# Storing the kept input gradient from GpSimd's queue in a planned S4 and FFN gradient kernel

## The chip, the cores and the metric

The kernel runs on one core of a Trainium2 chip, in one launch. The metric is the device time of a run in microseconds. Before the change three runs took 560.41, 562.75 and 563.41 us, so the median is 562.75.

## The reference

The reference is a small network and all its gradients. The input `A_u` (2048 rows of 512) is normalized; one branch is an S4 layer (a long convolution whose kernel comes from a complex diagonal recurrence, done with Fourier transforms), the other a feed-forward layer with 1792 inner columns; one gates the other.

```python
def _A_ref(u, A_re, A_im, B_re, B_im, C_re, C_im, log_dt, Dskip):
    dt = jnp.exp(log_dt)[:, None]
    A = A_re + 1j * A_im
    ...
    P = jnp.exp(logdA[:, :, None] * l[None, None, :])
    K = jnp.einsum("dn,dnl,dn->dl", Cc, P, dB).real
    ...
    return y + u * Dskip[None, None, :]      # y: u convolved with K, by FFT

def _B_ref(x, w1, w2):
    h = _silu(jnp.einsum("bsd,df->bsf", x, w1))
    return jnp.einsum("bsf,fd->bsd", h, w2)

xn = _layernorm(A_u)
out = A_u + _A_ref(xn, ...) * _silu(_B_ref(xn, B_w1, B_w2))

_out, _vjp = jax.vjp(_f, A_u, A_A_re, ..., A_Dskip, B_w1, B_w2)
return (out, *_vjp(grad_out))
```

The outputs are `out` and eleven gradients: those of the input, of the eight S4 parameter arrays and of the two weights.

## The kernel before

**How an order comes about.** The program is written twice. `body` runs once against a `Recorder`, which only notes each operation (so most operations have line L171, the line that emits them). `Plan` reads the recorded list, finds what depends on what, gives each operation a cost, and plays the engines forward; at each moment the ready operation with the smallest key goes next on its engine. The keys come from a backward pass (`backward`, how long before the end each operation is due), `ROUNDS` rounds of forward and backward from a start of noise named by `FROM`, and then from `NUDGES`, a list of small random shifts of keys that a search has kept. `FIRST` and `LAST` are the settings of `forward` in the rounds and in the last pass: in the signature of `forward` their five numbers are `hold`, `table`, `turn`, `shy` and `land`. A DMA is released no earlier than `latest[n] - hold`. ScalarE takes an operation whose activation table is loaded ahead of one whose table is not, as long as its key is less than `table` larger; `turn` does the same on TensorE for the form of the tiles. `shy` is what a copy must gain to leave its better engine, and `land` how long a transfer is taken to land. Then all operations are emitted in the order found, engine by engine, and each engine keeps that order.

**Copies without an engine.** Most copies out of PSUM are noted as `k.ev`, "any": the plan gives each to VectorE or to ScalarE.

**Stores.** `k.st` is a DMA start on GpSimd's queue (POOL); `k.nc.sync.dma_start` is one on SyncE's queue (SP). Both queues issue in their own order and stand still at an issue whose data or room is not ready.

**The stages**, in the names that the profile shows. *Head:* constants (`TF`, `TI`, `SEL`, `MK`, `FO`), `dt` and thirty exponentials `mag_all` on ScalarE, stored to `Md` by eight DMAs and reloaded as `mag`; the normalized rows `xn`, turned by TensorE into `XT`. The working area `AR` lies on the room of the head's tiles, so its first write waits for those eight stores. *Forward:* the S4 tables (`AR`, `sn`, `E`, `YD`, `W`, `Xr`, `KE`), four blocks of convolution by transforms (`ps_s` to `dA` forward, `ps_i` back, `S_b` the result) and the feed-forward layer (`ps_h` to `hT`, silu to `aT`, `ps_o` to `ob`). *Backward:* the gated rows are turned (`doT`), `gen_ffn_da` computes `ps_da` and `dhT` for eight chunks of 256 rows and then, for each chunk, two products `ps_dx`, the feed-forward share of the input's gradient; meanwhile `gen_conv_bwd` runs the transforms backward into `ds` and `gen_out` writes the first output (`go_x`). *Parameters:* `GE`, `Gb`, `ps_v`, `Vb`, `Tp`, `Tq` and `psS` are the S4 parameter gradients; `ps_w` the weight gradients, which read `hT` again as `h_in`. *End:* `gen_ln_bwd` joins the shares of the input's gradient through the normalization (`Gt`).

**Kept input gradient.** For the first `APART` = 5 chunks `ps_dx` cannot yet be added to `ds`. These ten tiles are copied to `pd_s` (one buffer) and stored in the DRAM tensor `Pd`; `gen_ln_bwd` reads them back as `pd_l`. For the other three chunks VectorE adds `ps_dx` to `ds` directly.

Of the kernel before, what the change touches and what calls it, by code (L numbers as in the profile page):

```python
# [180 lines left out]
class Plan:  # L181
# [5 lines left out]
    FROM, ROUNDS = (649172052, 1, 0), 5  # L187
    FIRST, LAST = (30000.0, 1500.0, 1500.0, 120.0, 3500.0), (30000.0, 1500.0, 1500.0, 120.0, 3500.0)
    NUDGES = [(2732807006, 5, 2000), (3483623756, 4, 500), (36678232, 7, 1000), (3625006935, 3, 100), (1835227684, 0, 100),
# [600 lines left out]
    def solve(self):  # L790
# [6 lines left out]
        for i in range(self.ROUNDS):  # L797
# [3 lines left out]
            if i < self.ROUNDS - 1:  # L801
                p = self.forward(key, latest, *self.FIRST)
        for seed, way, much in self.NUDGES:
            of = lambda n: self.noise(n, seed)
# [895 lines left out]
def gen_ffn_da(k, da):  # L1700
# [11 lines left out]
    for c in range(T // 2):  # L1712
# [26 lines left out]
        for t in range(2):  # L1739
# [4 lines left out]
            if c < k.apart:  # L1744
                pd = da.tile([P, D], BF16, name="pd_s", tag="pd_s", bufs=1)
# [326 lines left out]
```

## Time and profile before

| | |
|---|---|
| runs | 560.41, 562.75, 563.41 us, median 562.75 |
| the profiled execution's own time | 562.31 us |
| its span, first to last instruction | 560.6 us |
| mean granted TensorE clock | 0.991 |
| instructions | 14249 |

In a row of a group the columns are: line, engine, operation, output from input, size and type, count, then busy us and mean ns of one, then how long the engine stood idle before it and what ended that. In a timeline they are start and length in us. In the chain of waits they are start, length and what ran. An issue row gives the queue, the count, the size of one and the median us from issue to landing. PEld is the loading of weights into TensorE, beside the multiplication.

### The profile page before, as it was taken

The page shows a single profiled execution, that of the slowest core. Times are in us where ns is not written, and L with a number is a line of the kernel's source. Part 1 is how long each engine was busy: PE and PEld are TensorE (multiplying, and loading weights), DVE is VectorE, ACT ScalarE, POOL GpSimd, SP SyncE. Part 2 cuts the span into 40 slices and gives each one's busy share as a digit, 9 for nine tenths or more (in the row PEclk, how much of TensorE's full clock was granted, in tenths as well). Part 3 has the DMA queues.
Part 4 walks back from the last instruction along what each step waited for, and adds up shares of the span by engine and source line. Part 5 has one row for each costly group of instructions (what it writes and reads, how often), then busy time and mean ns, then how long its engine had stood idle before and what let it go on. Part 6 is the DMA issues. An engine that isn't in the chain of part 4 may idle for free.

```text
span 560.6 us, 14249 instructions
## 1 busy us (share of the span) xinstructions
PE 515.5 (92%) x5820; PEld 380.5 (68%) x5820; DVE 508.1 (91%) x866; ACT 432.0 (77%) x726; POOL 69.4 (12%) x138
## 2 busy tenths in 40 slices
PE   1698999999989997889999999999969999999997
PEld 1465677868657666565877667778657687778775
DVE  9989999999999799999999999649999999999932
ACT  8989899999989889989878878247367665785621
POOL 5131111100100100000000100000000303301142
PEclk9999999999999998999999999999989999999999
DMA  8996959997999999985498997997999999998893
GB/s 236 270 354 179 291 191 337 246 335 155 237 350 280 359 337 218 236 208 169 156 236 295 252 329 234 188 264 180 229 254 241 227 237 277 256 229 217 200 233 109
DMA packets 178882, 137.77 MB, mean 246 GB/s; under 512 B 125121, under 2 KB 158657, under 8 KB 176257
## 3 DMA queue, kind: packets, MB, share of 16 engines
q1 hardware_dynamic: 172384, 118.77, 82.5%
q0 software_dynamic: 6144, 17.83, 9.6%
q8 instruction: 45, 0.74, 0.5%
q10 hardware_dynamic: 288, 0.26, 0.2%
q14 instruction: 21, 0.16, 0.1%
HBM read 50.07 MB, written 56.63 MB: 190 GB/s over the span
## 4 chain that ended last, share of the span: by engine, by line
PE 58%; DVE 16%; ACT 13%; DMA 8%; issue 3%; SPq 2%; POOL 0%; DVEq 0%; ACTq 0%; POOLq 0%
PE ps_w L171 18%; PE ps_da L171 8%; PE ps_i L171 7%; PE ps_dx L171 6%; DMA dB<-dA 4%; PE ps_s L171 4%; PE ps_o L171 3%; ACT mag_all L171 3%; PE ps_h L171 3%; PE pt_t L171 3%; PE psS L171 3%; PE ps_v L171 2%; ACT dA L171 2%; DVE AR L171 2%; DVE dA L171 2%
## 5 line engine op out<-in xcount | busy, mean ns | idle before, releaser
L171 PEld LDWEIGHTS <-W 128*128 128x128 bf16 x952 | 88.1, 99 | 22.9 <-issue 7.4
L171 ACT CAST dA<-ps_s 128x512 bf16<-128x512 f32 x160 | 86.2, 641 | 9.2 <-PE ps_s L171 6.3
L171 PE MATMUL ps_o<-W,aT 128*128 128x512 bf16 x224 | 59.0, 379 | 2.9 <-ACT aT L171 2.9
L171 PEld LDWEIGHTS <-xn 128*128 128x128 bf16 x512 | 47.3, 99 | 20.1 <-DVE xn L171 13.0
L171 PE MATMUL ps_da<-doT,W 128*128 128x256 bf16 x448 | 59.7, 273 | 0.8 <-DVE doT L171 0.8
L171 PE MATMUL ps_h<-XT,W 128*128 128x256 bf16 x448 | 58.9, 277 | 1.3 <-DVE dA L171 0.8
L171 PE MATMUL ps_w<-YD,a_tok 128*128 128x512 bf16 x224 | 57.5, 382 | 0.0
L171 PE MATMUL ps_w<-dh_tok,xn 128*128 128x256 bf16 x448 | 57.1, 273 | 0.0
L171 ACT CAST Vb<-ps_v 128x336 bf16<-128x336 f32 x109 | 40.6, 459 | 21.2 <-PE ps_v L171 15.5
L171 PE MATMUL ps_dx<-W,dhT 128*128 128x512 bf16 x224 | 55.2, 379 | 0.0
L171 ACT CAST dB<-ps_i 128x512 bf16<-128x512 f32 x82 | 45.3, 647 | 4.5 <-PE ps_i L171 4.3
L171 DVE TENSOR_TENSOR dhT<-ps_da,dhT 128x512 bf16<-128x512 f32 x56 | 37.8, 685 | 6.1 <-PE ps_da L171 5.9
L171 PEld LDWEIGHTS <-TF 128*128 128x128 bf16 x416 | 28.5, 100 | 12.5 <-ACT TF L171 5.3
L171 PEld LDWEIGHTS <-YD 128*128 128x128 bf16 x576 | 28.4, 98 | 9.0 <-DVE YD L171 1.7
L171 PEld LDWEIGHTS <-dhT 128*128 128x128 bf16 x224 | 20.7, 98 | 20.1 <-issue 1.2
L171 PEld LDWEIGHTS <-a_tok 128*128 128x128 bf16 x224 | 21.3, 99 | 16.9 <-issue 0.5
L171 PEld LDWEIGHTS <-aT 128*128 128x128 bf16 x224 | 19.4, 98 | 19.5 <-ACT aT L171 3.4
L171 PE MATMUL ps_v<-Gb,YT 128*128 128x168 bf16 x256 | 31.1, 242 | 1.3 <-DVE Gb L171 0.7
L171 ACT CAST o<-ps_w 128x512 bf16<-128x512 f32 (+1 forms) x27 | 15.1, 559 | 20.9 <-PE ps_w L171 20.4
L171 PE MATMUL ps_s<-dB,F 128*64 128x512 bf16 x192 | 28.6, 400 | 2.8 <-DMA dB<-dA 1.7
L171 POOL DMA_DIRECT2D out_dram<-o x20 | 12.3, 616 | 142.8 <-ACT o L171 135.0
L171 ACT ACTIVATE sn<-AR 128x1920 bf16<-128x1920 int16 x16 | 28.7, 1870 | 0.0
(218 smaller groups left out, 1212.9 us busy)
## 6 DMA issues: line engine op xcount, KB each, us to landing
Yd<-YD SPq DMA_DIRECT2D x8, 1024.0 KB, 6.5
h_in<-Hd SPq DMA_DIRECT2D x11, 512.0 KB, 5.5
Ed<-E SPq DMA_DIRECT2D x8, 672.0 KB, 4.3
Eb<-Ed SPq DMA_DIRECT2D x8, 672.0 KB, 5.4
Hd<-hT POOLq DMA_DIRECT2D x8, 512.0 KB, 5.7
dhT<-Hd SPq DMA_DIRECT2D x8, 512.0 KB, 5.4
DHd<-dhT SPq DMA_DIRECT2D x8, 512.0 KB, 6.9
Md<-mag_all SPq DMA_DIRECT2D x8, 480.0 KB, 6.4
```

What stands on the lines that cost most here:

```text
L171: getattr(getattr(nc, engine), op)(*[on(a) for a in args], **{w: on(a) for w, a in kw.items()})
```

## The change

The store of `pd_s` goes through `k.st`, so from SP's queue to POOL's, and the plan's numbers are new: another start, four rounds instead of five, a `table` of 5000 instead of 1500, and 557 nudges instead of 663. The computation is the same.

```diff
@@ class Plan
-    FROM, ROUNDS = (649172052, 1, 0), 5
-    FIRST, LAST = (30000.0, 1500.0, 1500.0, 120.0, 3500.0), (30000.0, 1500.0, 1500.0, 120.0, 3500.0)
-    NUDGES = [(2732807006, 5, 2000), (3483623756, 4, 500), (36678232, 7, 1000), (3625006935, 3, 100), (1835227684, 0, 100),
...
+    FROM, ROUNDS = (99146811, 1, 1000), 4
+    FIRST, LAST = (30000.0, 5000.0, 1500.0, 120.0, 3500.0), (30000.0, 5000.0, 1500.0, 120.0, 3500.0)
+    NUDGES = [(1422119664, 3, 16000), (3699653561, 7, 2000), (2414858728, 4, 500), (342434683, 3, 4000), (3955565900, 7, 8000),
...
@@ gen_ffn_da
             if c < k.apart:
                 pd = da.tile([P, D], BF16, name="pd_s", tag="pd_s", bufs=1)
                 k.ev(pd[:], ps[:])
-                k.nc.sync.dma_start(k.Pd[:, 2 * c + t, :], pd[:])
+                k.st(k.Pd[:, 2 * c + t, :], pd[:])

**How it moves instructions.** Nearly every engine's order changes. Three places matter for what follows.

The first is the head on ScalarE, from the first table load to the exponentials. Before:

```order
L171 ACT_TABLE_LOAD
L171 ACTIVATE TF<-prod 128x2048
L171 ACT_TABLE_LOAD
L171 ACTIVATE dt<-ldt 128x512
L171 ACT_TABLE_LOAD
L171 ACTIVATE sf<-kf,mpi 128x128
L171 ACTIVATE sv<-kq,mpi 128x192
L171 ACT_TABLE_LOAD
L171 ACTIVATE mag_all<-lamr 128x8x64 x30
```

and with the change:

```order
L171 ACT_TABLE_LOAD
L171 ACTIVATE TF<-prod 128x2048 x2
L171 ACTIVATE sf<-kf,mpi 128x128
L171 ACTIVATE sv<-kq,mpi 128x192
L171 ACT_TABLE_LOAD
L171 ACTIVATE dt<-ldt 128x512
L171 COPY TI<-pt_t 128x1024
L171 ACTIVATE mag_all<-lamr 128x8x64 x30
```

The second `TF` and the sines now come ahead of the exponentials, two table loads stand in front of `mag_all` instead of four, and a `TI` copy has joined. On VectorE, what stands in front of `lamr`, which `mag_all` reads, was

```order
L171 TENSOR_SCALAR kq<-kk 128x64
L171 COPY TI<-pt_t 128x1024
L171 TENSOR_SCALAR kq<-kq 128x192
L171 TENSOR_SCALAR pj<-ip 128x1
L171 TENSOR_TENSOR lamr<-dt,par_Ar 128x512
```

and is

```order
L171 TENSOR_TENSOR rl<-xcst,pj 128x8
L171 COPY TI<-pt_t 128x1024
L171 TENSOR_TENSOR rl<-xcst,pj 128x12
L171 COPY TI<-pt_t 128x1024
L171 CAST rl<-pj 128x1
L171 TENSOR_TENSOR m_106<-pa,ia 128x4
L171 COPY TI<-pt_t 128x1024
L171 TENSOR_TENSOR MK<-rl,m_106 128x88
L171 TENSOR_TENSOR F_130<-sf,maskf 128x128
L171 TENSOR_TENSOR sv<-sv,maskf 128x192
L171 TENSOR_TENSOR lamr<-dt,par_Ar 128x512
```

so that two more `TI` copies and several small constants (three more `SEL` further up) now come first.

The second place is where the kept gradient is stored. On SP the first two of the ten stood so:

```order
L171 DMA dhT<-Hd 128x8x256
L171 DMA Pd<-pd_s 128x512
L171 DMA DHd<-dhT 128x1536
L171 DMA go_x<-in_A_u_dram 128x1024
L171 DMA sp_in<-Ud 128x4096
L171 DMA Pd<-pd_s 128x512
L171 DMA dhT<-Hd 128x6x256
L171 DMA go_x<-in_A_u_dram 128x1024
L171 DMA sp_in<-KXd 128x4096
```

and on POOL the stores now stand between those of the first output:

```order
L171 DMA out_dram<-go_x 128x1024
L171 DMA Pd<-pd_s 128x512
L171 DMA out_dram<-go_x 128x1024
L171 DMA Pd<-pd_s 128x512
L171 DMA out_dram<-go_x 128x1024
L171 DMA Pd<-pd_s 128x512
L171 DMA out_dram<-go_x 128x1024
L171 DMA Pd<-pd_s 128x512
L171 DMA out_dram<-go_x 128x1024
L171 DMA Pd<-pd_s 128x512 x2
L171 DMA out_dram<-dK 4x1x32
```

All ten have left SP; in POOL's order a `go_x` store follows most of them, and two stand side by side.

The third is SP's queue around the first two loads of `h_in`, which need the room of the weights and tiles that the last `ps_dx` reads. Before:

```order
L171 DMA DHd<-dhT 128x1536
L171 DMA Eb<-Ed 128x2688
L171 DMA_TRANSPOSE par<-in_A_A_re_dram 128x1x512
L171 DMA GE<-dKd 32x8x256
L171 DMA_TRANSPOSE par<-in_A_A_im_dram 128x1x512
L171 DMA h_in<-Hd 128x2048 x2
L171 DMA_TRANSPOSE YT<-Yd 128x8x128 x3
```

and now:

```order
L171 DMA DHd<-dhT 128x1536
L171 DMA GE<-dKd 32x8x256
L171 DMA_TRANSPOSE par<-in_A_A_re_dram 128x1x512
L171 DMA_TRANSPOSE YT<-Yd 128x8x128 x2
L171 DMA h_in<-Hd 128x2048 x2
L171 DMA Eb<-Ed 128x2688
L171 DMA_TRANSPOSE par<-in_A_A_im_dram 128x1x512
L171 DMA_TRANSPOSE YT<-Yd 128x8x128
```

One transposed `par` has moved behind `h_in`, and a pair of `YT` transposes ahead of it. On TensorE, between the last `ps_dx` and the first `h_in` transpose, there were 53 matmuls (`ps_v`, `psS`) and there are 80 (`psS`, `G`, `ps_v`). In the forward part, counted up to the first `doT` copy on VectorE and the last `S_b` on ScalarE, these numbers differ most:

| | VectorE before | now | ScalarE before | now |
|---|---|---|---|---|
| `hT<-ps_h` | 8 | 13 | 48 | 43 |
| `AR` from `AR` | 9 | 12 | 7 | 4 |
| `KE<-ps_e` | 12 | 26 | 36 | 22 |
| `Xr<-ps_k` | 21 | 13 | 11 | 19 |
| `S_b<-ps_i` | 6 | 3 | 10 | 12 |
| `ob<-ps_o` | 5 | 3 | 11 | 13 |
| table loads | | | 9 | 6 |

229 rows, old and new, of the table NUDGES are left out of this document.

## The prediction, on record before the run

> **What bounds the kernel now.** I read four views in this order: the page's first part, the busy time of the engines in four stretches, the chain of waits, and then the timelines of the two places where TensorE stands still.
>
> The first part of the page, busy time and share of the span for each engine:
>
> ```profile
> span 560.6 us, 14249 instructions
> PE 515.5 (92%) x5820; PEld 380.5 (68%) x5820; DVE 508.1 (91%) x866; ACT 432.0 (77%) x726; POOL 69.4 (12%) x138
> ```
>
> TensorE and VectorE both look full, which a mean over the program cannot separate. The busy time by stretch does; the cuts are the forward part (until the last work before the first ps_da), the backward part up to the last ps_dx, the hole behind it, and the rest. Columns: length, then PE, PEld, DVE, ACT, POOL busy us, the granted clock, DMA share, GB/s.
>
> ```profile
> 0.00:246.00 246.00, 209.79 (x2588) 154.01 (x2588) 232.31 (x393) 230.46 (x360) 31.21 (x69) 0.99 0.94 269
> 246.00:407.20 161.20, 159.90 (x1838) 115.33 (x1835) 144.38 (x210) 112.01 (x196) 6.73 (x13) 1.00 0.88 231
> 407.20:415.80 8.60, 4.12 (x55) 3.71 (x55) 8.60 (x16) 5.52 (x13) 0.00 (x0) 1.00 1.13 269
> 415.80:560.60 144.80, 141.65 (x1344) 107.44 (x1344) 122.83 (x250) 84.01 (x158) 31.42 (x56) 0.99 0.95 222
> ```
>
> In the first 246 us TensorE idles 36 us (246 - 209.79), while VectorE and ScalarE, which empty its PSUM banks, are busy 232.3 and 230.5 us: there those two set the pace, and equally. From 246 to 407 us TensorE is busy 159.9 of 161.2 us and sets it. In the 8.6 us that follow it stands idle half the time, and after that it is busy 141.7 of 144.8 us. The kernel is therefore two eviction engines, then TensorE with one hole.
>
> The chain of waits says what starts the first stretch:
>
> ```profile
> PE 58%; DVE 16%; ACT 13%; DMA 8%; issue 3%; SPq 2%; POOL 0%; DVEq 0%; ACTq 0%; POOLq 0%
> ...
> 10.54 15.71 ACT mag_all L171 x30
> 33.75 7.33 DMA mag<-Md
> 41.08 1.17 DVE AR L171
> ```
>
> The thirty exponentials (mag_all) begin at 10.54 us; their eight stores and one reload must land before the first table product AR at 41.08. POOL and its queue are at 0% of the chain.
>
> **The change, part by part.** *The ten stores.* They leave SP and go to POOL.
>
> ```profile
> L171 SPq DMA_DIRECT2D Pd<-pd_s x10: 319/353/725, 259.7 to 389.5; - x10
> SPq L171 <- ACT pd_s L171: 9.6, 5, 4.3
> Pd<-pd_s SPq DMA_DIRECT2D x10, 128.0 KB, 5.2
> out_dram<-o POOLq DMA_DIRECT2D x14, 128.0 KB, 5.0
> L171 POOL DMA_DIRECT2D out_dram<-gout x24: 540/540/541, 442.8 to 545.9; - x24
> ```
>
> SP gives up ten issues of about 0.35 us and 9.6 us of standing before pd_s; behind these in SP's order stand loads of dhT, sp_in and go_x. All ten lie between 259.7 and 389.5 us, in the stretch where TensorE is busy 159.9 of 161.2, so at most 1.3 us can be won there by earlier loads. The stores of the same 128 KB that POOL issues land in 5.0 us against 5.2. On POOL they cost more to issue: 540 ns for a smaller store, so some 0.2 us each later, 2 us over ten if nothing hid it; POOL is busy 6.7 us of the 161, so it has room. On POOL's order go_x stores stand behind them; the wait for such a store has two buffers of cover. I put this part at 0, with bounds of -1.3 and +2.
>
> A rule of the Trainium skill speaks against it (page "SBUF — State Buffer", section "SBUF: two separate sides"): while VectorE runs an operation in a two-port mode, GpSimd cannot write the descriptors of its DMA, so that the transfer seems blocked until VectorE ends. In this trace POOL's 24 gout issues take 540, 540 and 541 ns at the least, the median and the most, with VectorE nearly full beside them, so no such stall shows in the issue. By that rule the ten stores would start late, and that makes one of the rivals below.
>
> *The new plan.* FROM, ROUNDS, FIRST, LAST and NUDGES together reorder all engines. Three places decide.
>
> (1) The head. Four table loads up to mag_all become two, since table, the second number of FIRST, lets an operation wait 5000 instead of 1500 for its table's turn; but VectorE does more first.
>
> ```profile
> 3.31 1.91 ACT L171 ACTIVATE TF<-prod 128x2048 bf16<-128x2048 int16 x1 [0.81 <-DVE prod L171]
> 6.54 0.63 ACT L171 ACTIVATE dt<-ldt 128x512 bf16<-128x512 bf16 x1
> 8.48 0.40 ACT L171 ACTIVATE sf<-kf,mpi 128x128 f32<-128x128 int32 x1
> 8.79 0.44 ACT L171 ACTIVATE sv<-kq,mpi 128x192 f32<-128x192 int32 x1
> 9.24 1.28 ACT L171 ACT_TABLE_LOAD   x1
> 7.79 1.00 DVE L171 TENSOR_TENSOR lamr<-dt,par_Ar 128x512 f32<-128x512 bf16 x1
> L171 DVE TENSOR_TENSOR prod<-il,jf 128x1024 int32<-128x1024 int32 x2 | 2.4, 1222 | 1.3 <-POOL jf L171 1.3
> L171 DVE TENSOR_TENSOR SEL<-eq,own 128x512 bf16<-128x512 bf16 x3 | 1.2, 390 | 0.0
> L171 DVE COPY TI<-pt_t 128x1024 bf16<-128x1024 bf16 x4 | 2.7, 666 | 0.0
> L171 ACT COPY XT<-pt_t 128x1024 bf16<-128x1024 bf16 x3 | 3.3, 1115 | 0.0
> ```
>
> On ScalarE: the first TF now waits for both products, so it starts about 1.1 us later than 3.31, at 4.4. Then come two TF at 1.9 (8.2), sf and sv (some 0.7 together, 8.9), one load of 1.28 (10.2), dt (0.6, 10.8) and one TI copy (1.1, as the XT copy of its size, 11.9). On VectorE, ahead of lamr stand three more SEL (1.17) and two more TI copies (1.33) than before, and nine small ones of about 0.1 to 0.3 us (some 1.6): 4.1 us, less about 0.08 us by which short ones overlap, 3 to 4 us. lamr moves from 7.79 to between 10.9 and 11.9, and mag_all, one lamr (1.0) behind it, to 11.9 to 12.9. I take 12.2, the middle of both engines' answers: 1.7 us later than 10.54. The way from mag_all to the first AR is stores and a load on SP, the same in both orders, so AR starts 1.7 us later too: **+1.7**, bounds +0 (VectorE has evictions to do ahead of AR, as it now has four dA there) and +2.4.
>
> The first xn row, and with it TensorE's first ps_h, moves as well:
>
> ```profile
> 21.82 7.79 PE L171 MATMUL ps_h<-XT,W 128*128 128x256 bf16 x56 [0.23 <-DVE XT L171]
> ```
>
> Ahead of xn now stand three SEL, one TI, the small ones, two sp_t and one BN_STATS (of a TI copy's length each) that came behind it: 4 to 5 us, so ps_h starts at some 26 to 27 instead of 21.82. TensorE has 36 us of idle time in this stretch to hide it, and the work that VectorE pulled forward is not done later. A third of 4 us is what I let through: **+1.3**, bounds 0 and +5.
>
> (2) Evictions in the forward part. Counted in the order up to the first doT copy on VectorE and the last S_b on ScalarE, VectorE takes 5 hT and 3 AR more, 14 small KE more, 8 Xr, 3 S_b, 2 ob fewer, and the rest nearly cancels; ScalarE loses three table loads, 5 hT and 3 AR.
>
> ```profile
> L171 DVE CAST hT<-ps_h 128x512 bf16<-128x512 f32 x8 | 5.2, 683 | 0.0
> L171 DVE TENSOR_SCALAR AR<-AR 128x960 int32<-128x960 int32 x9 | 5.6, 651 | 0.0
> L171 DVE CAST Xr<-ps_k 128x336 bf16<-128x336 f32 x21 | 10.5, 502 | 1.5 <-PE ps_k L171 1.3
> L171 DVE CAST KE<-ps_e 128x32 bf16<-128x32 f32 x6 | 1.0, 187 | 1.5 <-ACT KE L171 1.5
> L171 ACT ACT_TABLE_LOAD x10 | 12.8, 1283 | 1.4 <-PEq L2056 1.2
> L171 ACT CAST hT<-ps_h 128x512 bf16<-128x512 f32 x48 | 27.2, 647 | 0.0
> L171 ACT ACTIVATE AR<-AR,quarter 128x960 int32<-128x960 int32 x7 | 7.7, 1116 | 2.5 <-DVE AR L171 2.5
> DVE KE L171 <- ACT KE L171: 2.7, 5, 0.7
> ```
>
> VectorE: 5 x 0.683 + 3 x 0.651 + 3.4 for KE (six of 0.187, the others of 0.29) - 8 x 0.502 - 5 x 0.68 + 2.7 for one G and YD chunk and the other pairs that move = about +4.1, some 3.7 with the overlap. ScalarE: -3 x 1.283 - 5 x 0.647 - 3 x 1.116 + 1.5 for the rest = about -8.9. Before, the two were even, so VectorE alone would now set the pace: +3.7. Against it stand the 2.7 us in which VectorE waited for ScalarE's KE (last row), since it now does these itself: **+1.0**. Bounds: +3.7, if VectorE's idle time stays; and -2.2, if the two share perfectly, (4.1 - 8.9)/2 with the overlap.
>
> (3) The hole behind the last ps_dx.
>
> ```profile
> 401.02 6.21 PE L171 MATMUL ps_dx<-W,dhT 128*128 128x512 bf16 x28
> 408.77 1.28 SPq L171 DMA_TRANSPOSE par<-in_A_A_im_dram  x1
> 410.15 1.00 SPq L171 DMA_DIRECT2D h_in<-Hd  x2
> 415.76 1.07 PE L171 MATMUL pt_t<-ident,h_in 128*128 128x128 bf16 x16 [3.15 <-DMA h_in<-Hd]
> ```
>
> The loads of h_in take the room of the tiles that ps_dx reads. It ends at 407.23; SP, busy with a GE load and a transposed par, issues h_in 2.9 us later; they land 5.6 us after that. In the new order one par goes behind h_in and a pair of YT transposes stands ahead of it. At best the 2.9 us go down to 0.4 (-2.5); at worst a YT pair is in the way and it grows by 0.9. I take **-0.8**.
>
> *The sum.* 1.7 + 1.3 + 1.0 - 0.8 + 0 = +3.2 us. The profiled execution took 562.31 us, 1.7 more than its span: 565.5. It is 0.44 below the median of the three runs, so against the median: 565.95, **566.0 us, slower by 0.6%**.
>
> **The rivals.** *The forward part shares.* ScalarE has 8.9 us less to do, and the planner chooses for each copy where it goes; if VectorE's waits for it shrink as much, the stretch gains 2.2 and the head costs 1.7: 562.3 us. For it: the two were loaded alike. Against: the copies have been dealt out, and VectorE got more.
>
> *Faster, because the hole closes.* Place: TensorE between the last ps_dx and the first h_in transpose, 8.6 us with 4.12 busy, so 4.5 idle. In the new order 80 small matmuls (psS, G, ps_v) stand there in place of 53, and one par fewer stands ahead of the loads; SP no longer stands before pd_s either. If that fills the hole, the forward part shares as above, and the head costs half of my 3.0, the time is 562.75 - 4.5 - 2.2 + 1.5 = 557.5 us. It decides once TensorE's added work there is as long as the landing of h_in (5.6 us). For it: TensorE's order at that place has changed in just this way, and ScalarE is relieved. Against: psS and ps_v wait for VectorE, which is busy for all of the 8.6 us in the stretch's row.
>
> *The stores starve on POOL.* pd_s has one buffer, so a store that is late holds the next copy, the copy a PSUM bank, and that ps_dx. VectorE's long operations there are these:
>
> ```profile
> L171 DVE TENSOR_TENSOR sp_in<-sp_in,dA 128x2048 bf16<-128x2048 bf16 x12 | 14.6, 1217 | 0.1
> ```
>
> The ten stores lay 14 us apart in the mean (259.7 to 389.5) and landed in 5.2; in the new order two stand side by side on POOL. If each waits for two such operations, 2.4 us, and two of them meet the next copy, 4.9 us come on top of the sum: 571 us. It decides from the point at which a store's issue and landing outlast the way to the next ps_dx. Against it: the level 540 ns above. This is the case that the page's rule leads to.
>
> **How the numbers follow.** The forecast (566.0) gets 0.45, its own range 563 to 570 from the bounds of the head and of VectorE's share. The starved stores get 0.08, the shared forward part 0.12, the closed hole 0.35. About 0.5% (2.8 us) is what a measurement of this kernel tells from no change: below 559.9 is faster, above 565.6 slower. Of the forecast's 0.45 some 0.41 lies above that bound and 0.04 within, with the starved stores and 0.01 of the shared case 0.50 slower; within it 0.04 + 0.09 + 0.02 = 0.15; faster 0.33 + 0.02 = 0.35. The range reaches from the closed hole with a hidden head, 556 (562.75 - 4.5 - 2.2), to the forecast with both upper bounds of the head and the evictions, 566 + 0.7 + 2.7 + 3.7 = 573.
>
> **What would show it.** Right: mag_all starting near 12.2 and the first AR near 43 us; the first ps_h after 25 us; the first ps_da at 248 us or later, with VectorE's idle time before it no smaller than 13.7 us (246 - 232.3) and ScalarE's clearly larger; h_in issued 2 us or so after the last ps_dx; pd_s without waits. Wrong: a first ps_da before 245 us (then the evictions share), TensorE's idle time between the last ps_dx and the first h_in transpose under 2 us (then the hole has closed), POOL issues of Pd well above 0.6 us or a wait of ps_dx for pd_s (then the rule holds), or a last stretch in which TensorE waits for VectorE, which my sum leaves out.

## The result and the profile after

Four runs of the changed kernel took 566.02, 567.55, 568.58 and 569.31 us, median 568.07, against 561.62 for before (four runs). The ratio is 1.0103, 95% interval 1.0063 to 1.0143, so the change costs 3.5 to 8 us, about 5.8 (561.62 x 0.0103); the two medians alone lie 6.5 us apart. The forecast was 566.0, or 0.6%.

The profiled run has a span of 566.9 us, 6.3 more than before. Its busy time by stretch, with cuts at the first `ps_da`, at the last `ps_dx`, at the first transpose of `h_in` and at the end (length, then PE, PEld, DVE, ACT, POOL busy us, clock, DMA share, GB/s):

```profile
0.00:251.00 251.00, 210.42 (x2573) 154.50 (x2573) 233.34 (x403) 221.95 (x345) 33.59 (x69) 0.99 0.91 265
251.00:409.70 158.70, 156.92 (x1771) 112.14 (x1771) 140.02 (x205) 105.83 (x176) 12.17 (x23) 1.00 0.85 223
409.70:416.70 7.00, 5.22 (x82) 4.91 (x82) 7.00 (x13) 4.45 (x13) 0.00 (x0) 1.00 1.01 197
416.70:566.90 150.20, 144.94 (x1397) 109.68 (x1397) 131.35 (x262) 91.48 (x178) 31.38 (x56) 1.00 1.00 230
```

The same first two cuts in before's trace (the other two rows stand in the prediction):

```profile
0.00:244.40 244.40, 208.19 (x2573) 152.58 (x2574) 230.71 (x390) 228.86 (x359) 31.21 (x69) 0.99 0.94 269
244.40:407.20 162.80, 161.50 (x1851) 116.75 (x1850) 145.98 (x213) 113.61 (x198) 6.73 (x13) 1.00 0.89 231
```

The first `ps_da` starts 6.6 us later (244.4 to 251.0). From there to the end both kernels take the same time: 560.6 - 244.4 = 316.2 us before, 566.9 - 251.0 = 315.9 now. The whole loss lies in the forward part. There VectorE is busy 2.6 us longer (230.71 to 233.34) and idle 4.0 us longer (13.7 to 17.7), while ScalarE has 6.9 us less to do.

The head came out as worked out. From the timelines of ScalarE, VectorE and TensorE:

```profile
12.20 2.19 ACT L171 ACTIVATE mag_all<-lamr 128x512 bf16<-128x512 f32 x4 [0.50 <-DVE lamr L171]
42.76 2.23 DVE L171 TENSOR_TENSOR AR<-tau,xcst 128x960 int32<-128x960 f32 x2 [2.56 <-DMA mag<-Md]
25.63 3.61 PE L171 MATMUL ps_h<-XT,W 128*128 128x256 bf16 x19 [1.11 <-DVE XT L171]
```

`mag_all` starts at 12.20 and `AR` 1.7 us later than 41.08. What grew behind them are VectorE's waits up to the first `ps_da` (us in total, times, longest), first in before and then with the change:

```profile
DVE KE L171 <- ACT KE L171: 2.7, 5, 0.7
...
DVE AR L171 <- DMA Gr<-in_grad_out_dram: 0.7, 1, 0.7
```

```profile
DVE KE L171 <- ACT KE L171: 5.8, 10, 1.5
DVE AR L171 <- DMA Gr<-in_grad_out_dram: 3.7, 1, 3.7
```

`KE` is a table that twelve copies for each of four blocks bring out of the banks `ps_e`; it is stored (`Kd`), and the plan lets `Gr`, the loaded output gradient, be loaded only behind the last of these stores. VectorE now waits ten times for a `KE` copy of ScalarE's, and it stands still for 3.7 us before the first product with `Gr`.

### The profile page after: what moved, and what is told of

Same layout as the page of the kernel before. It is cut to its first block, busy times and chain, and to the rows that moved or that the text cites. A ratio compares the mean times of both kernels' runs of the same rounds, so it can differ in the third digit from the quotient of the medians.

```text
span 566.9 us, 14271 instructions
## 1 busy us (share of the span) xinstructions
PE 517.5 (91%) x5820; PEld 381.2 (67%) x5820; DVE 511.7 (90%) x879; ACT 423.7 (75%) x710; POOL 77.1 (14%) x148
## 5 line engine op out<-in xcount | busy, mean ns | idle before, releaser
L171 PEld LDWEIGHTS <-W 128*128 128x128 bf16 x952 | 87.3, 98 | 22.0 <-issue 6.4
L171 ACT CAST dA<-ps_s 128x512 bf16<-128x512 f32 x151 | 81.7, 638 | 6.4 <-PE ps_s L171 4.3
L171 PE MATMUL ps_h<-XT,W 128*128 128x256 bf16 x448 | 59.1, 277 | 3.3 <-DVE XT L171 1.6
L171 PE MATMUL ps_o<-W,aT 128*128 128x512 bf16 x224 | 58.1, 383 | 3.6 <-DVE dB L171 2.1
L171 PE MATMUL ps_da<-doT,W 128*128 128x256 bf16 x448 | 59.9, 273 | 0.6 <-DVE doT L171 0.6
L171 PEld LDWEIGHTS <-xn 128*128 128x128 bf16 x512 | 47.7, 99 | 18.5 <-DVE xn L171 12.4
L171 PE MATMUL ps_w<-YD,a_tok 128*128 128x512 bf16 x224 | 57.0, 379 | 0.0
L171 ACT CAST Vb<-ps_v 128x336 bf16<-128x336 f32 x116 | 43.3, 469 | 16.4 <-PE ps_v L171 12.9
L171 PE MATMUL ps_w<-dh_tok,xn 128*128 128x256 bf16 x448 | 55.1, 273 | 0.0
L171 PE MATMUL ps_dx<-W,dhT 128*128 128x512 bf16 x224 | 54.9, 379 | 0.1
L171 ACT CAST dB<-ps_i 128x512 bf16<-128x512 f32 x78 | 43.0, 618 | 11.8 <-PE ps_i L171 11.8
L171 DVE TENSOR_TENSOR dhT<-ps_da,dhT 128x512 bf16<-128x512 f32 x56 | 38.0, 697 | 5.7 <-PE ps_da L171 5.0
L171 PEld LDWEIGHTS <-TF 128*128 128x128 bf16 x416 | 29.8, 103 | 13.8 <-ACT TF L171 6.4
L171 ACT CAST o<-ps_w 128x512 bf16<-128x512 f32 (+1 forms) x30 | 17.0, 566 | 29.0 <-PE ps_w L171 23.6
L171 PEld LDWEIGHTS <-aT 128*128 128x128 bf16 x224 | 20.3, 98 | 22.2 <-issue 4.9
L171 PEld LDWEIGHTS <-dhT 128*128 128x128 bf16 x224 | 20.9, 98 | 21.1 <-issue 1.2
L171 PE MATMUL ps_s<-dB,F 128*64 128x512 bf16 x192 | 28.4, 387 | 7.2 <-DMA dB<-dA 4.1
L171 ACT ACTIVATE dhT<-dhT 128x2048 bf16<-128x2048 bf16 (+1 forms) x16 | 27.3, 1735 | 10.2 <-DMA dhT<-Hd 7.2
L171 PEld LDWEIGHTS <-YD 128*128 128x128 bf16 x576 | 28.4, 98 | 8.1 <-DVE YD L171 3.1
L171 PE MATMUL ps_v<-Gb,YT 128*128 128x168 bf16 x256 | 31.4, 239 | 1.0 <-DMA YT<-Yd 0.9
L171 PEld LDWEIGHTS <-a_tok 128*128 128x128 bf16 x224 | 20.8, 98 | 16.4 <-issue 0.2
L171 ACT ACTIVATE sn<-AR 128x1920 bf16<-128x1920 int16 x16 | 29.4, 1856 | 0.9 <-DVE AR L171 0.9
```

Of the source, the lines that this page charges most:

```text
L171: getattr(getattr(nc, engine), op)(*[on(a) for a in args], **{w: on(a) for w, a in kw.items()})
```

## The experiments

All kernels use one device: the program solves the plan with before's numbers (`Before`, stores on SP) or with the change's (`After`, stores on POOL), and `replay` then emits the operations in a given order (`wish`), each copy on a given engine (`eng`), in the plan's banks where they are free. `kept` are the ten stores, `queue` the engine that issues them. With a plan's own order `replay` gives the instructions of that kernel. The first `ps_da` is read from one profiled execution of each kernel, the ratio from 4 to 12 runs of it.

| run | first `ps_da`, us | ratio to before, 95% interval |
|---|---|---|
| the change | 251.0 | 1.0103 (1.0063 to 1.0143) |
| e1, before's order, stores on POOL | 242.9 | 1.0011 (0.9992 to 1.0030) |
| e2, the change's order, stores on SP | 250.8 | 1.0093 (1.0064 to 1.0122) |
| e3, forward part of before, rest of the change | 244.5 | 1.0001 (0.9978 to 1.0024) |
| e4, forward part of the change, rest of before | 252.5 | 1.0098 (1.0067 to 1.0128) |
| e5, head of before | 252.1 | 1.0114 (1.0085 to 1.0144) |
| e6, `Gr` products behind evictions | 250.3 | 1.0088 (1.0058 to 1.0118) |
| e7, `KE` engines of before | 248.8 | 1.0064 (1.0035 to 1.0092) |
| e8, `hT` and `AR` engines of before | 258.6 | 1.0242 (1.0207 to 1.0277) |
| e9, e6 and e7 together | 246.9 | 1.0036 (1.0017 to 1.0054) |
| e10, head of before, `AR` first | 256.0 | 1.0169 (1.0143 to 1.0195) |
| e11, e9 and e10 together | 252.7 | 1.0137 (1.0111 to 1.0162) |
| e12, before with the change's `KE` engines | 248.0 | 1.0100 (1.0070 to 1.0130) |

Two things limit how far the middle column can be read. The change, e2 and e4 run the same order up to the first `ps_da`, and it comes at 250.8 to 252.5 us; before, e1 and e3 share the other one, and it comes at 242.9 to 244.5. So a difference of less than about 1.7 us between two single profiles says nothing by itself. And in the profiles of e2, e4, e6 and e8 the granted TensorE clock was lower in the head, 0.80 up to the first `AR`, where the change's profile and before's have 1.00:

```profile
0.00:42.80 42.80, 21.98 (x208) 19.36 (x209) 38.97 (x119) 36.61 (x55) 16.31 (x47) 1.00 0.85 276
```

```profile
0.00:43.00 43.00, 22.42 (x197) 19.26 (x198) 38.74 (x119) 36.58 (x55) 16.69 (x47) 0.80 0.85 278
```

The first row is the change's, the second e6's; the clock is the third number from the end. In e2, which has the lower clock and the change's order, the first `ps_da` is not later than in the change (250.8 against 251.0); what the clock costs was not isolated.

### The queue against the order: e1 and e2

```diff
-plan, made = planned(After, "gpsimd")
+plan, made = planned(Before, "sync")         # e1; e2 keeps the line above
 wish, eng, bank = plan.best.sequence, plan.best.eng, plan.best.slot
+queue = "gpsimd"                             # e1; "sync" in e2
 for n in kept:
     rec.ops[n] = (queue,) + rec.ops[n][1:]
```

> The order of before on every engine, only the ten stores of pd_s issued by GpSimd at the same places. Theory (the queue is worth nothing): within 2 us of before, TensorE's last stretch and first ps_da as before (244.4 us), each Pd issue near 0.54 us. Rival (the stores starve on POOL or hold pd_s): 3 to 9 us slower, with ps_dx or the next pd_s copy waiting for a Pd store. Rival (SP freed of ten issues and of 9.6 us of standing): faster by 1 us or more.

> The order of the change on every engine, only the ten stores of pd_s issued by SyncE at the same places. Theory (the order alone makes the loss): as slow as the change, ratio 1.007 to 1.014 to before, first ps_da near 251 us. Rival (the queue makes the loss): back at before, ratio below 1.004.

The stores alone on POOL leave the time where it was (1.0011, the interval holds 1). The order alone, with the stores back on SP, is as slow as the change (1.0093). The rows of the stores in e1:

```profile
L171 POOL DMA_DIRECT2D Pd<-pd_s x10: 540/540/561, 260.4 to 367.5; - x10
```

The issues take 540 to 561 ns while VectorE is busy 146.1 of 162.9 us of that stretch, and they land in 4.9 us (median) against 5.2 on SP. The other engines' only wait that the trace puts to the stored tile is one of 0.7 us before a `dA` copy, and before has the same one. ScalarE's idle time ahead of its nine copies to `pd_s` is 10.3 us in both (8.4 + 1.9 in before, 3.6 + 6.7 in e1). So the queue costs nothing that this measurement finds (the interval of e1 leaves room for 1.7 us), and the order accounts for the loss.

### Which part of the order: e3 and e4

```diff
+old, new = planned(Before, "sync"), planned(After, "gpsimd")
+(x, _), (plan, made) = (old, new)            # e4: (new, old)
+cut = next(i for i, n in enumerate(x.best.sequence) if x.writes(n) == "ps_da")
+early = set(x.best.sequence[:cut])
+wish = x.best.sequence[:cut] + [n for n in plan.best.sequence if n not in early]
+eng = [(x if n in early else plan).best.eng[n] for n in range(plan.N)]
```

> All operations that before's order has ahead of the first ps_da run in before's order and on before's engines, everything else in the order of the change; stores of pd_s on GpSimd. Theory (the loss lies wholly ahead of the first ps_da): first ps_da at 244 to 245 us and the time of before within 2 us (560 to 563). Rival (the part behind the first ps_da loses too, or catches up what the forward part lost only because it started late): 565 us or more.

> All operations that the change's order has ahead of the first ps_da run in that order, everything else in the order of before; stores of pd_s on SyncE. Theory: first ps_da at 250 to 252 us and a time 5 to 8 us above before (567 to 570). Rival (the part behind makes the loss): within 2 us of before.

Both came out on the side of the theory. Before's forward part with the change's rest gives before's time (1.0001), the change's forward part with before's rest gives the change's (1.0098).

### The parts of the forward loss, one by one: e5 to e8

```diff
+cut = next(i for i, n in enumerate(old.best.sequence) if old.writes(n) == "AR")     # e5, else as in e3
...
+late = [n for n in wish if plan.writes(n) == "AR" and "Gr" in plan.reads(n)][:4]    # e6
+last = [n for n in wish[wish.index(late[0]):] if plan.writes(n) == "dB" and eng[n] == "DVE"][3]
+wish = [n for n in wish if n not in late]
+wish[wish.index(last) + 1:wish.index(last) + 1] = late
...
+for n in plan.other:                         # e7; in e8 ("hT", "AR")
+    if plan.writes(n) in ("KE",):
+        eng[n] = old.best.eng[n]
```

> All operations that before's order has ahead of the first AR run in before's order, the rest in the order of the change. Theory (terms 1 of the sum: the head costs 1.7 and its late ps_h 1.3): first AR back at 41.1 us, first ps_da 1.7 to 3 us earlier than the 251.0 of the change, time ratio to before 1.004 to 1.007. Rival (a wait further on, the load of Gr, swallows the gain): first AR at 41.1 but first ps_da still near 251 and a ratio of 1.009 or more.

> The order of the change, but on VectorE the first four products AR<-Gr stand behind the next four dB and the one dA evictions in place of between them. Theory (VectorE standing 3.7 us before Gr holds evictions that TensorE waits for): that wait falls below 1 us, first ps_da 2 to 3.7 us earlier, ratio 1.004 to 1.006. Rival (VectorE's sum of work sets the stretch and the idle time reappears at another wait): first ps_da within 1 us of 251, ratio 1.009 or more.

> The order of the change, but each copy KE<-ps_e on the engine that before gave it (12 on VectorE in place of 26). Theory (each change of engine between KE copies costs a wait): VectorE's waits for ScalarE's KE fall from 5.8 to about 2.7 us and the first ps_da comes 2 to 3 us earlier, ratio near 1.005. Rival (only the last group of KE, which Gr waits for, matters, and its changes of engine are the same in both orders): the waits fall but the first ps_da moves by less than 1 us.

> The order of the change, but each hT<-ps_h and each integer AR copy on the engine that before gave it, so VectorE has 5 hT and 3 AR less (about 5.4 us) and ScalarE as many more. Theory of the prediction (VectorE alone sets the pace of the forward part): first ps_da about 3 to 4 us earlier, ratio 1.002 to 1.005. Rival (single waits set it, VectorE's added work is not the price): VectorE's idle time grows by as much as its work falls, first ps_da within 1 us of 251, ratio 1.009 or more.

*e5* did not do what it was built for. Operations that the change's order has ahead of `AR` and before's has not came in between, so the first `AR` started at 42.2 and not at 41.1. It says nothing of the head's price.

*e6* took the wait for `Gr` away, but the first `ps_da` came only 0.7 us earlier, with the lower clock in the head of its profile; VectorE's waits up to there are now

```profile
DVE KE L171 <- ACT KE L171: 5.8, 10, 1.5
DVE dA L171 <- PE ps_s L171: 3.0, 4, 1.5
```

so the idle time comes back before `dA`, 3.0 us in place of 0.9. This is nearer to the rival. By itself the interval (1.0058 to 1.0118) does not part it from the change.

*e7* moved the first `ps_da` by 2.2 us, as the theory said, with VectorE's waits

```profile
DVE KE L171 <- ACT KE L171: 3.9, 5, 1.5
DVE AR L171 <- DMA Gr<-in_grad_out_dram: 3.0, 1, 3.0
DVE dA L171 <- ACT dA L171: 2.6, 1, 2.6
```

The number of waits for `KE` is back at five. But VectorE also lost 14 copies, and its busy time up to the first `ps_da` fell by the same 2.2 us (233.34 to 231.17), while its idle time in sum stayed at 17.6. So the profile puts 2.2 us on the `KE` copies on VectorE; it does not tell their waits from their work. The interval (1.0035 to 1.0092) overlaps with the change's, so this step, too, is not shown by the times of e7 alone.

*e8* is the clearest miss. It took 3.9 us of work off VectorE (233.34 to 229.48) and the stretch became 7.6 us longer:

```profile
DVE KE L171 <- ACT KE L171: 5.9, 10, 1.5
DVE E L171 <- ACT sn L171: 4.8, 4, 2.0
DVE YD L171 <- ACT sn L171: 4.4, 4, 1.8
```

The last two rows are 9.2 us of waits for `sn`; the change has 0.3 us in them. The tables run from VectorE (`AR`) to ScalarE (`sn`) and back (`E`, `YD`); an `hT` or `AR` copy that ScalarE takes ahead of a `sn` delays it, and VectorE waits. This is how I read the two rows; which copy delays which `sn` was not tried. That VectorE took these copies was right for this order.

### What adds up: e9 to e12

e9 holds the edits of e6 and e7. e10 is e5 with the first `AR` set directly behind before's head, and e11 puts the edits of e6, e7 and e10 together. e12 goes the other way, from before:

```diff
+first = old.best.sequence[cut]               # e10, e11
+wish = old.best.sequence[:cut + 1] + [n for n in plan.best.sequence if n not in early and n != first]
...
+(plan, made), (new, _) = planned(Before, "sync"), planned(After, "gpsimd")          # e12
+for n in plan.other:
+    if plan.writes(n) == "KE":
+        eng[n] = new.best.eng[n]
```

> Both edits that were tried singly: each KE copy on the engine that before gave it, and VectorE's first four products AR<-Gr behind the next five evictions. The KE edit alone gave a first ps_da 2.2 us earlier, the other one 2 us between the last ps_i and the first store of S_b. Theory (the two are separate waits and add up): first ps_da at 246 to 247.5 us, ratio to before 1.002 to 1.005. Rival (they are one slack, or the second is taken back behind): first ps_da at 248.3 or later, ratio as with the KE edit alone (1.0064) or more.

> The head of before as in the earlier run, but now the first AR follows it at once on VectorE, ahead of the dA evictions that the change's order has before it. Theory (the 1.7 us by which AR starts later go through to the end): first AR at 41.1 us, first ps_da at 249 to 249.6, ratio 1.004 to 1.008. Rival (the start of AR has slack behind it): first AR at 41.1 and the first ps_da at 250.5 or later, ratio 1.009 or more.

> The three edits together: head of before with AR at its place, KE engines of before, the products AR<-Gr behind the evictions. Theory (the loss of 6.6 us ahead of the first ps_da is the head, the KE waits and the Gr wait): first ps_da at 244 to 246 us, ratio 0.999 to 1.003. Rival (the head gives nothing): first ps_da as with the two edits without it, within 0.6 us.

> The order and the queue of before, but each KE copy on the engine that the change gave it (26 on VectorE in place of 12). Theory (the changes of engine between KE copies cost by themselves, whatever the order around them): VectorE's waits for ScalarE's KE rise from 2.7 to about 5 us or more, first ps_da 1.5 to 2.5 us later than before, ratio 1.002 to 1.005. Rival (they cost only in the order of the change): first ps_da within 0.8 us of before, ratio below 1.002.

*e9* came out as the theory had it: the first `ps_da` at 246.9 and a ratio of 1.0036, so the two edits together take back 4.1 of the 6.6 us, more than the 2.2 and 0.7 us that they gave singly. Of the edits to the change's order, e9 is the only one whose interval lies below the change's. VectorE's busy time up to there is before's (230.72 against 230.71); the 2.5 us that are left are idle time.

*e10 and e11* do start `AR` at 41.2 and 40.8, and lose. From ScalarE's timeline in e10:

```profile
45.03 0.58 ACT L171 CAST dA<-ps_s 128x512 bf16<-128x512 f32 x1 [3.77 <-PE ps_s L171]
...
51.20 3.51 ACT L171 ACTIVATE sn<-AR 128x1920 bf16<-128x1920 int16 x2
```

In the change's own trace the same `sn` starts earlier, although its `AR` is later:

```profile
45.42 3.50 ACT L171 ACTIVATE sn<-AR 128x1920 bf16<-128x1920 int16 x2
```

With before's head in front, ScalarE's order reaches the first `sn` only after evictions that TensorE delivers late, 5.8 us behind the change's. In e10 the granted TensorE clock was also down to 0.52 and 0.63 from 44 to 46 and from 46 to 48 us (1.00 in the change's profile); how much of the lateness that makes was not isolated. The expectation that the head's 1.7 us would come back failed in both, but what these runs measure is the seam between two orders. The head's own price stays open.

*e12*: the same 14 copies cost before's order too. The first `ps_da` moved by 3.6 us (2.2 in e7, a difference within the scatter) and the time by 1.0%, more than the 0.2 to 0.5% of the theory. The theory expected the wait on the other engine: VectorE's waits for ScalarE's `KE` were to rise from 2.7 to 5 us or more and rose to 4.0. Here it is mainly ScalarE that waits, first in before and then in e12:

```profile
ACT KE L171 <- DVE KE L171: 1.7, 4, 0.6
```

```profile
ACT KE L171 <- DVE KE L171: 8.8, 9, 3.3
```

One of these waits is 2.4 us long, since the copies on VectorE stand in line behind table products:

```profile
82.67 1.75 DVE L171 TENSOR_TENSOR AR<-YD,H 128x3072 bf16<-128x3072 bf16 x1
84.33 0.38 DVE L171 CAST KE<-ps_e 128x32 bf16<-128x32 f32 x3
```

```profile
84.75 0.32 ACT L171 CAST KE<-ps_e 128x192 bf16<-128x192 f32 x1 [2.40 <-DVE KE L171]
```

In before ScalarE did ten copies of this block in 2.17 us without leaving them:

```profile
81.01 2.17 ACT L171 CAST KE<-ps_e 128x256 bf16<-128x256 f32 x10 [0.19 <-PE ps_e L171]
```

VectorE also has 2.5 us more work here (230.71 to 233.19), so e12 shows the price of where the copies go and not of the waits alone. No kernel of the study beats before: e1 and e3 equal it, and of the edits to the change's order e9 is the fastest.

## Why the prediction was right, and where its sizes were off

*The stores.* Costed at nothing, with bounds of -1.3 and +2: e1 gives 1.0011, 0.6 us. The traces of e1 and of the change show no wait of `ps_dx` for a store, so the starved stores did not come. The Trainium skill (page "SBUF — State Buffer", section "SBUF: two separate sides") lets such a store stand blocked while VectorE holds the shared port; the issues of 540 to 561 ns in e1, and landings of at most 6.6 us against 8.5 from SP's queue in before, show no such block in this kernel. The trace does not tell in which mode VectorE's operations ran beside these stores, so the rule itself is not tested.

*The head.* Two starts were right to the tenth: `mag_all` at 12.20 (forecast 12.2) and `AR` 1.7 us later (forecast +1.7). `ps_h` came at 25.63, a little ahead of the 26 to 27 worked out. That these 1.7 and the 1.3 for `ps_h` go through to the end was assumed, and no run shows it.

*The evictions of the forward part.* This is the term that was mis-sized. From the first `AR` to the first `ps_da` the prediction had 1.3 + 1.0 = 2.3 us more; the profiles show 203.3 and 208.2 us, 4.9 more. Before and now:

```profile
41.10:244.40 203.30, 186.03 (x2393) 135.70 (x2391) 192.84 (x273) 190.75 (x304) 16.59 (x22) 0.98 0.94 265
```

```profile
42.80:251.00 208.20, 188.44 (x2369) 135.15 (x2366) 194.38 (x285) 185.34 (x290) 17.28 (x22) 0.98 0.93 262
```

VectorE's work in it grew by 1.5 us (192.84 to 194.38), where the prediction counted 3.7, and its idle time grew by 3.4 (10.5 to 13.8), where the prediction took 2.7 off. Two steps of it failed. The first credited 2.7 us because VectorE "now does these itself", meaning the `KE` copies. It does only 26 of 48 and not all, so its waits for ScalarE's copies doubled in number and rose from 2.7 to 5.8 us; e7 puts 2.2 us on those copies, and e12 shows them to be expensive in before's order too. The second held VectorE's sum of work for the pace. By that, giving the `hT` and `AR` copies back to ScalarE should have gained 3 to 4 us; e8 shows that it cost 7.6 us. The unforeseen wait for `Gr` comes on top: SP issues the four loads one behind the other, and the first product starts 8.7 us behind the first issue:

```profile
200.76 4.71 SPq L171 DMA_DIRECT2D Gr<-in_grad_out_dram  x4
...
209.50 1.29 DVE L171 TENSOR_TENSOR AR<-Gr,G 128x1024 bf16<-128x1024 bf16 x2 [3.70 <-DMA Gr<-in_grad_out_dram]
```

In before two other loads stand between the first and the second, and the first product started 5.3 us behind the first issue, without a wait (a later one waits 0.7 us):

```profile
197.65 0.55 SPq L171 DMA_DIRECT2D Gr<-in_grad_out_dram  x1
198.31 0.86 SPq L171 DMA_DIRECT2D YD<-Od  x2
...
202.92 1.28 DVE L171 TENSOR_TENSOR AR<-Gr,G 128x1024 bf16<-128x1024 bf16 x2
```

So the delay is 1.7 us at the first `AR`, 3.1 at the first load of `Gr`, 6.6 at the first product with it and 6.6 at the first `ps_da`. That does not make this wait the price of half the loss: taken away alone (e6) it gave 0.7 us, and with the `KE` edit beside it 1.9 (248.8 in e7, 246.9 in e9). Whether spacing the loads would do the same was not tried.

*The sign of the waits.* That VectorE's idle time ahead of the first `ps_da` would be no smaller than 13.7 us and ScalarE's clearly larger held: 17.7, and 29.0 after 15.5. The sign contradicts the sum, though, which took VectorE's waits to shrink.

*The hole.* Forecast -0.8; TensorE's idle time there fell from 4.5 to 1.8 us, which is the mark that the prediction set for "the hole has closed". `h_in` is issued 1.3 us behind the last `ps_dx` (2.9 before), with `psS`, `G` and `ps_v` in between, as that rival had it. But from the first `ps_da` to the end the kernel gained only 0.3 us. Up to the last `ps_dx` that part is 4.1 us shorter and the hole 1.6, but the last stretch is 5.4 longer: 80 matmuls fewer run ahead of the last `ps_dx`, 27 more in the hole and 53 more behind it. In the last stretch TensorE now idles 5.3 us (150.2 - 144.94) in place of 3.15. A part of that are waits that the sum left out, from TensorE's waits in this stretch, where before has none for these two:

```profile
PE ps_v L171 <- DMA YT<-Yd: 0.9, 2, 0.5
PE psS L171 <- DVE Tp L171: 0.8, 1, 0.8
```

So two of the marks that the prediction set for being wrong did come, the closed hole and a last stretch in which TensorE waits for VectorE; both are small here (0.3 us in all, and one wait of 0.8).

*The sum.* Forecast +3.2 us, measured 5.8 with an interval of 3.5 to 8. The direction and the place were right, the size short by the forward waits. The direction rests in part on luck: that the head's 3.0 us go through was assumed, and the 1.0 us for the evictions came out of two steps that failed. Of the 6.6 us there, e9 takes back 4.1 (`KE` copies and the `Gr` products), to within the 1.7 us by which single profiles of one order differ; the 2.5 that are left are not assigned.

## What to carry to other kernels

When a planner's numbers change together with one line, test the line at a fixed order first: here the line was worth nothing and the new order everything. A count of work by engine did not price the order. Most of the price (4.1 of 6.6 us) went away with two small edits: one chose the engines for the copies of one tile, the other moved four products so that nothing stood behind their wait for a load. Before counting a shift of copies to another engine as relief, check that it takes all of the copies and not half of them.

## What the runs showed that was not expected

Fourteen copies of 0.19 to 0.55 us moved from ScalarE to VectorE cost before's order 1.0% of its time, as much as the whole change. Each copy writes its own columns of `KE`, yet where the engine changes most copies wait for the last one on the other engine (17 waits in e12, 9 in before). The code shows that they share the tile and, in two groups, a bank `ps_e`; which of the two makes them wait was not tried.
